# A recurrence with two expert layers on one core: the scans of every second window in another slot, and one PSUM bank emptied in another order

## The chip, the cores and the metric

The kernel runs on one core of a Trainium2 chip. The metric is device time in microseconds (us) of one execution of the program; lower is better. Five engines work side by side, each through its own queue in order: TensorE (PE, its weight loads shown as PEld), VectorE (DVE), ScalarE (ACT), GpSimd (POOL) and SyncE (SP, which here issues the DMA transfers).

## The reference

`r, k, v, w, a, b` have the shape (4, 8, 768, 40): 32 independent (batch, head) pairs, 768 time steps, 40 features. Each pair has a 40x40 state.

```python
for t in range(768):
    y[:, :, t] = einsum('bhd,bhde->bhe', r_t, state)
    Sa = einsum('bhde,bhe->bhd', state, a_t)
    state = state * w_t[:, :, None, :] - outer(Sa, b_t) + outer(v_t, k_t)
x  = y as (3072 tokens, 320)
h  = x @ w_in                                  # 320 -> 1024
s  = h * softmax(h)
x2 = (layer_norm(s) * g_ln) @ w_out            # 1024 -> 320
h2 = x2 @ w_in2                                # 320 -> 2048
out = (max(h2, 0) + alpha * min(h2, 0)) @ w_out2
```

## The kernel before, in words

The 768 steps are cut into 12 windows of 64 steps, and each window into two chunks of 32, so there are 24 chunks. Inside a chunk the recurrence is solved with matrices: the decays are turned into running products by scans along time, keys and values are scaled by them, a strictly triangular 32x32 matrix per pair is formed, its inverse gives the corrections, and the state goes from one chunk to the next.

The program has two phases. **Phase 1** (up to about 743 us of the profiled execution) walks the 24 chunks in 24 *slots*. Slot g computes chunk g (`stage_x`, `stage_u`, `stage_uf`, `stage_st`, `stage_g2`, `stage_s`, `stage_y`, in this order), and beside it the first expert layer of earlier chunks (`mlp_tasks`), the decoding of weights from 64-bit words (`dec`) and the preparation of later windows. **Phase 2** is the second expert layer. The change touches phase 1 alone.

Each four slots form a group; with `W, c4 = divmod(g, 4)` the comments below call c4 = 0 the first slot of a group, c4 = 1 its second, and so on. During group W two windows are prepared, v = 2W+2 and u = 2W+3, which are the four chunks of the next group; for W = 0 to 4 both exist. The preparation of a window has these steps:

- `prep_load` (lines 224 to 230) loads the decays `wt`; `kb_load` (232) loads the keys and b (`kbf`, in two halves); `load_a` (239) clears a part of XS on POOL (line 245) and loads a.
- `check` (250): four ACT passes over the decays that look for values out of range. For windows below 4 it is called from within the scans.
- `prep_scan(w, pe)` (260), once for each half pe: on DVE a clamp (line 279), a small memset, two scans (lines 283 and 287) and a reciprocal between them. They yield the running products H and their inverses F. An odd window makes H first.
- `prep_kb` (304): kbf times F, two DVE products per half (line 309). `prep_a` (312): XS times H, two POOL products per chunk (line 318).
- `gen1(g, half)` (320): 64 PE matmuls per call (line 332) put a chunk's pair products into one PSUM bank, `pg`. After half 1 the bank is emptied in eight pieces of 32x256: four masked products on DVE into XS (line 342), and four negated copies on ACT (line 347), into `lraw` (a part of LMN) or, for chunks 0 to 3, into GR.
- `inverse(W+1)` (350) needs the `lraw` of all four chunks. It begins with a DVE transpose (line 374), goes on as a chain of small DVE products and sums (lines 362, 366, 391), with a part on POOL, and closes with a transpose (395). It is spread over the third and fourth slots of the group. The next group's first slot needs its result in `stage_u` (line 510).
- `trans` (464): PE transposes of kbf, whose copies (472, 473) fill KBS.

The order on PE is the order of the program text. On the other engines the compiler orders the instructions by their place in the text and by what is ready. `fill_tasks` says what goes at which letter within a slot; `slot` calls the letters: a, `pre`, b, `stage_u`, `stage_uf`, c, `stage_st`, `stage_g2` half 0, x, d, `stage_g2` half 1, e, `stage_s`, f, `stage_y`, z. The block `pre` stands right behind `stage_x` and the letter a; its DVE instructions are held behind the last sums of the state (line 550) of the slot before.

Other lines that are spoken of: 550, the DVE sums of the state into VUS, which `stage_s` waits for; 678 (`lnl`), a DVE step between the first expert layer's transposes and its second product (686 to 688, `po`); 691 (`xs`), the ACT copy that empties that product, and 700 (`ptx`), PE transposes of xs, which stand at the head of the next slot's PE queue; 602 and 606, the chunk's output; 714 to 723, decoding of weights (DVE, ACT, DVE, POOL).

Of the kernel before, what the change touches and what calls it, by code (L numbers as in the profile page):

```python
# [12 lines left out]
AF = mybir.ActivationFunctionType  # L13
# [13 lines left out]
NP = 4  # L27
TA, TB = ('0z', '0z', '1a', '1a'), ('2z', '2z', '3a', '3a')
CA, CB = ('3c', '3d'), ('d', 'd')
PA, PB = ('0x','0d','0e','0f'), ('1d','1e','1f','1z')  # L30
RES = 2
LAG, ND4 = 2, 4
PR, SM, TM = (10, 32), 2, 121
DA, KP = (1,), (1,)
PA0, PB0 = ('0x','0d','0e','0f'), ('1d','1e','1f','1z')
TA0 = ('0z', '0z', '1a', '1a')
TAIL = "s2 n0 w2 t0 s1 u0 a0 w3 b0 s1 n1 w4 o0 s1 t1 s1 u1 a1 w5 s1 b1 s1 n2 o1 s1 w6 t2 s1 u2 a2 x w7 s1 b2 s1 n3 o2 s1 t3 s1 u3 b3 s2 o3"
SB, LA, LB, LC, LD, KA, KB = 'd', 'x', 'x', 'c', 'a', 'b', 'b'
DK = (1, 1)
NI = 18  # L40
ZF = (1, 1, 1, 1)
# [7 lines left out]
def tile_kernel(ctx: ExitStack, tc: tile.TileContext, w_fm, a0_fm, a_fm, kb_fm, r_fm, v_fm, v_tm,  # L49
                w1_in, w1_out, g_ln, w2_in, w2_out, alpha, ident_d, mask_d, tri_d, r, k, v, w, a, b, w1_nat, out,  # L50
                manual=True):
    nc = tc.nc
# [59 lines left out]
    GR = ca.tile([128, 32, 48], F32, name="GR")  # L112
# [49 lines left out]
    st = {}  # L162
# [69 lines left out]
    def kb_load(w):  # L232
        kbf = st[w]["kbf"] = b2.tile([104, 16, 2, 2, 32], F32, name="kbf")
        for pe in range(2):
            ss = slice(pe * 8, pe * 8 + 8)
            nc.sync.dma_start(out=kbf[:, ss], in_=kb_fm[w][:, ss])

    def load_a(g):
        w, c = divmod(g, 2)
        x = XS[g % 6]  # L240
        for e, r0 in EO:
            if g < 6:
                nc.sync.dma_start(out=x[0:104, e], in_=a0_fm[g, e])
                continue
            nc.gpsimd.memset(x[64 * e:32 + 96 * e, e], 0.0)
            nc.sync.dma_start(out=x[r0:r0 + 40, e], in_=a_fm[w, c, e])
# [13 lines left out]
    def prep_scan(w, pe):  # L260
        s = st[w]
        wt = s["wt"][pe]
        if w < 4:
            check(w, pe)
        if pe == 0:
            s["F"] = [None, None]
        H3 = s["H"][:, pe * 8:pe * 8 + 8, :]
        Ht = H3.rearrange("p s k -> p (s k)")
        if w < 2:
            wc = m1.tile([104, 521], F32, name="wc", tag=("lnh", "lnl", "Y", "P")[2 * w + pe])  # L270
            Ft = m2.tile([104, 520], F32, name="F", tag="xt")
        else:
            wc = b3.tile([104, 521], F32, name="wc", tag="wf")
            Ft = b3.tile([104, 520], F32, name="F", tag="wf")
        F3 = Ft.rearrange("p (s k) -> p s k", k=65)
        s["F"][pe] = F3
        wv = wt[:, 0:520].rearrange("p (s k) -> p s k", k=65)[:, :, 1:65]
        wz = wc[:, 0:520].rearrange("p (s k) -> p s k", k=65)
        nc.vector.tensor_scalar(out=wz[:, :, 1:65], in0=wv, scalar1=W_MAX, scalar2=W_MIN, op0=ALU.min, op1=ALU.max)
        nc.vector.memset(wc[:, ::65], 0.0)  # L280

        def fwd(d):
            nc.vector.tensor_tensor_scan(out=Ht, data0=wc[:, 0:520], data1=d[:, 0:520], initial=0.0,  # L283
                                         op0=ALU.mult, op1=ALU.add)

        def rev(d):
            nc.vector.tensor_tensor_scan(out=Ft[:, ::-1], data0=wc[:, 520:0:-1], data1=d[:, 520:0:-1],
                                         initial=0.0, op0=ALU.mult, op1=ALU.add)

        if w % 2 == 0:  # L290
            rev(D1)
            nc.vector.reciprocal(out=resets(Dx, 0)[:, :, 0:1], in_=F3[:, :, 0:1])
            fwd(Dx)
            if w:
                if pe == 0:
                    s["rs"] = b1.tile([104, 16], F32, name="rs")
                nc.vector.tensor_tensor(out=s["rs"][:, pe * 8:pe * 8 + 8],
                                        in0=st[w - 1]["H"][:, pe * 8:pe * 8 + 8, 64], in1=F3[:, :, 0], op=ALU.mult)
        else:
            fwd(D1)  # L300
            nc.vector.reciprocal(out=resets(Dx, 1)[:, :, 64:65], in_=H3[:, :, 64:65])
            rev(Dx)

    def prep_kb(w, pe):
        s = st[w]
        for i in range(2):
            o = s["kbf"][:, pe * 8:pe * 8 + 8, :, i, :]
            eng = nc.vector if (i not in KP if w < 2 else DK[w % 2]) else nc.gpsimd
            st["kb1"] = eng.tensor_tensor(out=o, in0=o, in1=s["F"][pe][:, :, 1:65].rearrange("p s (c t) -> p s c t", c=2),  # L309
                              op=ALU.mult)  # L310

    def prep_a(g, *pes):
        w, c = divmod(g, 2)
        x = XS[g % 6]
        for e, r0 in EO:
            o = x[r0:r0 + 40, e, pes[0]:pes[-1] + 1].rearrange("p a s t -> p (a s) t")
            h = st[w]["H"][r0:r0 + 40, pes[0] * 8:pes[-1] * 8 + 8, c * 32:c * 32 + 32]
            (nc.vector if w < 2 and e in DA else nc.gpsimd).tensor_tensor(out=o, in0=o, in1=h, op=ALU.mult)  # L318

    def gen1(g, half):  # L320
        w, c = divmod(g, 2)
        x = XS[g % 6]
        kbf = st[w]["kbf"]
        if half == 0:
            st["pg1"] = ps_at.tile([128, 8, 2, 32], F32, name="pg", tag="at")
        pg = st["pg1"]
        wait(st["slot"], "gen%d%d" % (g % 4, half))
        for p in range(half * 4, half * 4 + 4):
            for pe in range(2):
                for i in range(2):  # L330
                    o = 64 * pe + 32 * i
                    nc.tensor.matmul(pg[o:o + 32, p], lhsT=kbf[:, pe * 8 + p, c, i, :], rhs=x[0:104, :, pe, p, :],
                                     start=True, stop=True)
            pace(0.19, 188)
        if half == 0:
            return
        c4 = g % 4
        for e in range(2):
            q = 64 * e
            for pe in range(2):  # L340
                o = 64 * pe
                nc.vector.tensor_tensor(out=x[q:q + 32, e, pe], in0=pg[o:o + 32, :, e],  # L342
                                        in1=mask[o:o + 32].unsqueeze(1).to_broadcast([32, 8, 32]), op=ALU.mult)
                r = q + 32 * pe
                to = (GR[r:r + 32, c4 * 8:c4 * 8 + 8, 47:15:-1] if g < 4 else
                      st["lraw"][r:r + 32, c4 * 8:c4 * 8 + 8, :])
                nc.scalar.activation(out=to, in_=pg[o + 32:o + 64, :, e], func=AF.Copy, scale=-1.0)  # L347


    def inverse(W):  # L350
# [460 lines left out]
    def fill_tasks(g):  # L811

        W, c4 = divmod(g, 4)
        pre, at = [], {}
        for n, places in ((2 * W + 1, TA if W else TA0), (2 * W + 2, TB)):
            for q, (c, x) in enumerate(places):
                if int(c) == c4 and n < NW:
                    at.setdefault(x, []).append(lambda n=n, q=q: trans(n, q))
        late = []

        def add(q, *fs):
            at.setdefault(q, []).extend(fs)
        w = 2 * W + 4
        if w < NW:
            if c4 == 2:
                add(LA, lambda: prep_load(w), lambda: load_a(2 * w))
            for c, x, pe in ((CA[0][0], CA[0][1], 0), (CA[1][0], CA[1][1], 1)):
                if int(c) == c4 and w > 3:
                    add(x, lambda pe=pe: check(w, pe))
            if c4 == 3:  # L830
                add(LB, lambda: kb_load(w), lambda: load_a(2 * w + 1))
        v = 2 * W + 2
        if c4 == 0 and v < NW:
            pre += [lambda: prep_scan(v, 0), lambda: prep_scan(v, 1)]
            add(KA, lambda: prep_kb(v, 0), lambda: prep_kb(v, 1), lambda: prep_a(2 * v, 0, 1),
                lambda: prep_a(2 * v + 1, 0, 1))
        u = 2 * W + 3
        if u < NW:
            if c4 == 0:
                add(LC, lambda: prep_load(u), lambda: load_a(2 * u))  # L840
                if u > 3:
                    add(CB[0], lambda: check(u, 0))
                    add(CB[1], lambda: check(u, 1))
                add(SB, lambda: prep_scan(u, 0), lambda: prep_scan(u, 1), lambda: prep_a(2 * u, 0, 1))
            if c4 == 1:
                add(LD, lambda: kb_load(u), lambda: load_a(2 * u + 1))
                add(KB, lambda: prep_kb(u, 0), lambda: prep_kb(u, 1), lambda: prep_a(2 * u + 1, 0, 1))
            for n, places in ((2 * W + 2, PA if W else PA0), (2 * W + 3, PB if W else PB0)):
                for f, (c, q) in zip(gen_tasks(n), places):
                    if int(c) == c4:  # L850
                        add(q, f)
        return pre, late, at
# [568 lines left out]
```

## Time and profile before

| | |
|---|---|
| three runs | 1130.83, 1130.81, 1122.72 us |
| median | 1130.81 us |
| the profiled execution | 1134.54 us, of which the span of the trace is 1132.8 us |
| phase 1 | to about 743 us |

A slot is read here from one copy of PX into XP (line 500) to the next; the starts of the 24 copies in the trace are, in us:

| group | first slot | second | third | fourth |
|---|---|---|---|---|
| W = 0 | 44.9 | 99.4 | 136.5 | 163.1 |
| W = 1 | 189.3 | 233.5 | 263.3 | 288.8 |
| W = 2 | 311.2 | 347.4 | 375.9 | 401.6 |
| W = 3 | 427.3 | 463.5 | 496.2 | 519.9 |
| W = 4 | 546.3 | 582.6 | 607.9 | 634.1 |
| W = 5 | 655.7 | 681.2 | 707.0 | 725.6 |

A row of a timeline gives start and duration in us, engine, line, operation, output and inputs, the number of instructions merged, and in brackets how long the engine sat idle before it and what it waited for.

### The profile page before, as it was taken

To read this page: it belongs to the slowest core of one execution; us is meant where nothing else is said; L and a number is where in the kernel's file an instruction comes from. 1 tells how busy PE (TensorE), PEld (TensorE's weight loads), DVE (VectorE), ACT (ScalarE), POOL (GpSimd) and SP (SyncE) were. 2 spreads that over 40 slices of the span, in tenths; PEclk is the share of its full clock that TensorE was granted. 3 is DMA by queue.
4 is the path that set the end of the run, shared out by engine and by line. 5 is a ranking of instruction groups with operands and counts; after the bars stand their busy time and mean duration, and the time that the engine had idled before them with its cause. 6 is when DMAs were issued, how large, how long until landed. Compare 5 with 4: busy or idle time off the path is not lost.

```text
span 1132.8 us, 38016 instructions
## 1 busy us (share of the span) xinstructions
PE 982.7 (87%) x16456; PEld 815.6 (72%) x16456; DVE 740.3 (65%) x1455; ACT 551.9 (49%) x1274; POOL 481.6 (43%) x505
## 2 busy tenths in 40 slices
PE   7777784799878878797878888999999999999997
PEld 3454452677766767576767776888988999999897
DVE  8783899778987788868877955466433333444443
ACT  3446563666757665666476657666212121212121
POOL 6467544453434334443344335245333333333332
PEclk8788787888988888779889989999999999999999
DMA  6443344444334433443334334355102020201000
GB/s 172 105 133 108 102 125 117 98 120 113 85 103 119 113 78 103 111 122 81 100 97 118 110 92 112 111 158 179 36 1 70 1 71 1 70 1 48 1 24 15
DMA packets 104690, 99.74 MB, mean 88 GB/s; under 512 B 38084, under 2 KB 83908, under 8 KB 104516
## 3 DMA queue, kind: packets, MB, share of 16 engines
q1 hardware_dynamic: 104516, 97.24, 31.6%
q8 instruction: 131, 2.15, 0.8%
q14 instruction: 43, 0.35, 0.1%
HBM read 71.78 MB, written 25.43 MB: 86 GB/s over the span
## 4 chain that ended last, share of the span: by engine, by line
PE 50%; DVE 23%; ACT 9%; issue 7%; POOL 5%; DMA 5%; SPq 0%; DVEq 0%; POOLq 0%; ACTq 0%
PE ph L1078 15%; PE acc L1096 5%; PE acc L1097 5%; PE acc L1098 5%; PE h L633 4%; DMA kbf<-in_kb_fm_dram 3%; DVE LMN L366 2%; DVE tmp L362 2%; DVE VUS L550 2%; PE py L598 2%; DVE H L283 2%; PE po L686 2%; PE pf L533 2%; DVE kbf L309 1%; PE po L688 1%
## 5 line engine op out<-in xcount | busy, mean ns | idle before, releaser
L1085 POOL TENSOR_TENSOR gll<-gt,gh 128x512 fp32r<-128x512 f32 (+1 forms) x112 | 128.3, 1146 | 223.7 <-ACT gh L1084 222.6
L653 DVE TENSOR_SCALAR gt<-ph,al 128x512 f32<-128x512 f32 (+1 forms) x112 | 75.5, 674 | 190.1 <-PE ph L1078 189.9
L1084 ACT CAST gh<-gt 128x512 fp32r<-128x512 f32 (+1 forms) x112 | 62.5, 559 | 255.1 <-DVE gt L654 217.0
L633 PE MATMUL h<-w1h,xt 128*128 128x512 f32 x240 | 99.0, 461 | 11.0 <-ACT h L642 11.0
L318 POOL TENSOR_TENSOR XS<-XS,H 40x512 f32<-40x512 f32 (+1 forms) x48 | 66.7, 1395 | 91.5 <-DVE H L283 55.2
L1096 PE MATMUL acc<-w2h,gh 128*128 128x320 f32 x288 | 89.0, 309 | 0.0
L1097 PE MATMUL acc<-w2l,gh 128*128 128x320 f32 x288 | 89.0, 309 | 0.0
L1098 PE MATMUL acc<-w2h,gll 128*128 128x320 f32 x288 | 88.9, 309 | 0.0
L586 POOL TENSOR_TENSOR YS<-YS,mask 64x512 f32<-64x512 f32 x48 | 62.0, 1291 | 55.6 <-ACT YS L585 53.7
L686 PE MATMUL po<-wo1h,lnh 128*128 128x320 f32 x192 | 70.7, 368 | 6.8 <-DVE lnl L678 6.7
L217 PE MATMUL busy<-busy 128*128 128x512 bf16 x231 | 70.2, 458 | 2.2 <-POOL lims L129 1.3
L654 DVE SCALAR_TENSOR_TENSOR gt<-ph,gt 128x512 f32<-128x512 f32 (+1 forms) x112 | 68.8, 615 | 3.7
L688 PE MATMUL po<-wo1h,lnl 128*128 128x320 f32 x192 | 64.6, 336 | 0.2 <-DVE lnl L678 0.2
L562 PE MATMUL pss<-ident,VUS 40*40 40x40 f32 x1472 | 43.8, 217 | 24.1 <-DVE VUS L550 7.7
L633 PE MATMUL h<-w1l,xt 128*128 128x512 f32 x144 | 64.7, 449 | 0.0
L687 PE MATMUL po<-wo1l,lnh 128*128 128x320 f32 x192 | 64.6, 337 | 0.0
L366 DVE TENSOR_TENSOR LMN<-LMN,tmp 128x87 f32<-128x87 f32 (+8 forms) x135 | 60.8, 450 | 2.7
L362 DVE TENSOR_TENSOR tmp<-LMN,LMN 128x87 f32<-128x87 f32 (+8 forms) x135 | 59.9, 443 | 2.7
L562 PEld LDWEIGHTS pss<-ident,VUS 40*40 40x40 f32 x1472 | 37.5, 130 | 33.5 <-issue 14.4
L342 DVE TENSOR_TENSOR XS<-pg,mask 32x256 f32<-32x256 f32 x96 | 40.0, 416 | 32.9 <-ACT LMN L347 23.4
L633 PEld LDWEIGHTS h<-w1h,xt 128*128 128x128 f32 x240 | 47.3, 207 | 18.1 <-ACT h L642 11.1
L1078 PE MATMUL ph<-w1h,w2h 128*128 128x512 f32 x180 | 59.3, 394 | 0.0
(213 smaller groups left out, 2711.6 us busy)
## 6 DMA issues: line engine op xcount, KB each, us to landing
kbf<-in_kb_fm_dram SPq DMA_DIRECT2D x24, 416.0 KB
x2d<-x SPq DMA_DIRECT2D x24, 320.0 KB
xd<-Y SPq DMA_DIRECT2D x24, 256.0 KB
xt<-xd SPq DMA_DIRECT2D x12, 512.0 KB
raw<-in_w_in_dram SPq DMA_DIRECT2D x20, 256.0 KB
wt<-in_w_fm_dram SPq DMA_DIRECT2D x24, 211.7 KB
raw<-in_w_in_dram SPq DMA_DIRECT2D x8, 512.0 KB
raw<-in_w_out_dram SPq DMA_DIRECT2D x16, 256.0 KB
```

What stands on the lines that cost most here:

```text
L362: eng.tensor_tensor(out=tv[:, a - rows[0][0]:b - rows[0][0]], in0=M[:, a:b, s:s + 1].to_broadcast(sh), in1=l.unsqueeze(1).to_broadcast(sh) ...
L366: r = eng.tensor_tensor(out=o, in0=o, in1=tv[:, a - rows[0][0]:b - rows[0][0]], op=ALU.add)
L562: nc.tensor.matmul(p_[o:o + 40, p, :], lhsT=vn[o:o + 40, e, pe * 8 + p, :], rhs=ident[o:o + 40, o:o + 40], start=True, stop=True)
L633: nc.tensor.matmul(st["h"][:, ns], lhsT=l, rhs=r, start=j == 0, stop=j == len(ops) - 1)
L653: nc.vector.tensor_scalar(out=tmp, in0=h, scalar1=0.0, scalar2=al, op0=ALU.min, op1=ALU.mult)
L686: nc.tensor.matmul(po, lhsT=lh[:, k], rhs=wo1h[:, k], start=k == 0, stop=False)
L688: nc.tensor.matmul(po, lhsT=ll[:, k], rhs=wo1h[:, k], start=False, stop=k == K1 - 1)
L1078: nc.tensor.matmul(p, lhsT=l, rhs=r, start=j == 0, stop=j == len(ops) - 1)
L1085: nc.gpsimd.tensor_tensor(out=gll, in0=t, in1=f32(gh), op=ALU.subtract)
L1096: nc.tensor.matmul(acc, lhsT=gh[:, cs], rhs=oh, start=f == 0, stop=False)
L1097: nc.tensor.matmul(acc, lhsT=gh[:, cs], rhs=ol, start=False, stop=False)
L1098: nc.tensor.matmul(acc, lhsT=gll[:, cs], rhs=oh, start=False, stop=f == K2 - 1)
```

## The change

Two edits. The scans of window u (both halves) leave letter d of the group's first slot and stand in `pre` of the second slot. The POOL products of chunk 2u, which stood behind them, go to letter b of the second slot, in front of those of chunk 2u+1. The four `gen1` calls of window u, which stood at d, e, f and z of the second slot, stand at e, f, z and z. The loads and the checks of windows above 3 stay; for window 3 the checks go along with the scans, which call them. In `gen1` the eight pieces of the bank are no longer emptied in turn by DVE and ACT: the four ACT copies come first in the text, then the four DVE products.

```diff
-PA, PB = ('0x','0d','0e','0f'), ('1d','1e','1f','1z')
+PA, PB = ('0x','0d','0e','0f'), ('1e','1f','1z','1z')
...
-PA0, PB0 = ('0x','0d','0e','0f'), ('1d','1e','1f','1z')
+PA0, PB0 = ('0x','0d','0e','0f'), ('1e','1f','1z','1z')
...
         for e in range(2):
             q = 64 * e
             for pe in range(2):
+                o, r = 64 * pe, q + 32 * pe
+                to = (GR[r:r + 32, c4 * 8:c4 * 8 + 8, 47:15:-1] if g < 4 else
+                      st["lraw"][r:r + 32, c4 * 8:c4 * 8 + 8, :])
+                nc.scalar.activation(out=to, in_=pg[o + 32:o + 64, :, e], func=AF.Copy, scale=-1.0)
+        for e in range(2):
+            q = 64 * e
+            for pe in range(2):
                 o = 64 * pe
                 nc.vector.tensor_tensor(out=x[q:q + 32, e, pe], in0=pg[o:o + 32, :, e],
                                         in1=mask[o:o + 32].unsqueeze(1).to_broadcast([32, 8, 32]), op=ALU.mult)
-                r = q + 32 * pe
-                to = (GR[r:r + 32, c4 * 8:c4 * 8 + 8, 47:15:-1] if g < 4 else
-                      st["lraw"][r:r + 32, c4 * 8:c4 * 8 + 8, :])
-                nc.scalar.activation(out=to, in_=pg[o + 32:o + 64, :, e], func=AF.Copy, scale=-1.0)
...
-                add(SB, lambda: prep_scan(u, 0), lambda: prep_scan(u, 1), lambda: prep_a(2 * u, 0, 1))
             if c4 == 1:
+                pre += [lambda: prep_scan(u, 0), lambda: prep_scan(u, 1)]
                 add(LD, lambda: kb_load(u), lambda: load_a(2 * u + 1))
-                add(KB, lambda: prep_kb(u, 0), lambda: prep_kb(u, 1), lambda: prep_a(2 * u + 1, 0, 1))
+                add(KB, lambda: prep_kb(u, 0), lambda: prep_kb(u, 1), lambda: prep_a(2 * u, 0, 1),
+                    lambda: prep_a(2 * u + 1, 0, 1))
```

Here SB was the letter d, LD is a and KB is b.

## Rows read from the trace of the kernel before

**Rows 1.** The page: busy time and share per engine; then the chain's shares by engine

```profile
PE 982.7 (87%) x16456; PEld 815.6 (72%) x16456; DVE 740.3 (65%) x1455; ACT 551.9 (49%) x1274; POOL 481.6 (43%) x505
...
PE 50%; DVE 23%; ACT 9%; issue 7%; POOL 5%; DMA 5%; SPq 0%; DVEq 0%; POOLq 0%; ACTq 0%
```

**Rows 2.** Windows by slot: length; busy PE, PEld, DVE, ACT, POOL; clock; DMA share; GB/s

```profile
44.90:99.40 54.50, 39.95 (x1175) 25.19 (x1173) 45.05 (x81) 27.34 (x61) 30.29 (x20) 0.84 0.36 106
99.40:136.50 37.10, 29.58 (x636) 18.53 (x634) 22.17 (x41) 19.33 (x45) 22.80 (x24) 0.80 0.37 94
...
189.30:233.50 44.20, 28.79 (x654) 23.50 (x655) 35.89 (x74) 26.01 (x59) 22.06 (x22) 0.81 0.38 92
233.50:263.30 29.80, 24.94 (x633) 20.25 (x631) 21.93 (x44) 21.00 (x53) 13.75 (x17) 0.89 0.49 127
...
311.20:347.40 36.20, 26.31 (x643) 22.20 (x642) 30.94 (x58) 21.78 (x56) 17.08 (x18) 0.80 0.35 94
347.40:375.90 28.50, 23.65 (x639) 19.37 (x637) 19.32 (x42) 20.39 (x50) 12.65 (x16) 0.96 0.52 136
...
427.30:463.50 36.20, 26.29 (x643) 22.18 (x642) 30.79 (x57) 21.75 (x55) 17.06 (x18) 0.80 0.35 94
463.50:496.20 32.70, 29.49 (x639) 24.12 (x637) 20.53 (x42) 20.58 (x51) 12.62 (x16) 0.75 0.46 117
...
546.30:582.60 36.30, 26.71 (x645) 21.98 (x644) 30.74 (x58) 21.78 (x56) 17.89 (x18) 0.81 0.35 94
582.60:607.90 25.30, 22.84 (x635) 19.30 (x634) 16.51 (x36) 18.05 (x44) 10.64 (x14) 0.93 0.44 115
```

**Rows 3.** Timeline of DVE, slot 8: start, duration, instruction, idle before and its releaser

```profile
336.44 1.24 DVE L283 TENSOR_TENSOR_SCAN H<-wc,D 104x520 f32<-104x520 f32 x1 [0.27 <-ACT H L257]
...
344.12 2.15 DVE L287 TENSOR_TENSOR_SCAN F<-wc,Dx 104x520 f32<-104x520 f32 x1
```

**Rows 4.** Timeline of ACT in slot 8

```profile
343.10 0.43 ACT L691 COPY xs<-po 128x320 f32<-128x320 f32 x1
```

**Rows 5.** Timeline of PE at the end of slot 8 and into slot 9

```profile
343.58 0.90 PE L700 MATMUL ptx<-ident,xs 128*128 128x128 f32 x3 [6.20 <-ACT xs L691]
344.13 0.78 PE L633 MATMUL h<-w1h,xt 128*128 128x512 f32 x1
...
350.28 0.40 PE L633 MATMUL h<-w1h,xt 128*128 128x512 f32 x1
```

**Rows 6.** Timeline of POOL in slots 8 and 9

```profile
344.00 3.26 POOL L318 TENSOR_TENSOR XS<-XS,H 40x512 f32<-40x512 f32 x2
...
357.74 3.17 POOL L318 TENSOR_TENSOR XS<-XS,H 40x512 f32<-40x512 f32 x2 [7.28 <-DMA XS<-in_a_fm_dram]
```

**Rows 7.** Groups by line, whole kernel (busy, mean ns, idle before)

```profile
L279 DVE TENSOR_SCALAR wc<-wt 104x512 f32<-104x512 f32 x24 | 12.6, 526 | 1.8 <-DMA wt<-in_w_fm_dram 1.8
...
L318 POOL TENSOR_TENSOR XS<-XS,H 40x512 f32<-40x512 f32 (+1 forms) x48 | 66.7, 1395 | 91.5 <-DVE H L283 55.2
```

**Rows 8.** Timeline of DVE in slot 9 and at the start of slot 10

```profile
352.00 0.69 DVE L678 TENSOR_TENSOR lnl<-ptr,lnh 128x512 fp32r<-128x512 f32 x1 [2.41 <-ACT lnh L677]
352.79 1.29 DVE L309 TENSOR_TENSOR kbf<-kbf,F 104x512 f32<-104x512 f32 x2
...
357.55 2.31 DVE L309 TENSOR_TENSOR kbf<-kbf,F 104x512 f32<-104x512 f32 x2 [0.24 <-DMA kbf<-in_kb_fm_dram]
359.89 0.49 DVE L550 TENSOR_TENSOR VUS<-pst,VUS 40x320 f32<-40x320 f32 x1
...
367.00 0.42 DVE L342 TENSOR_TENSOR XS<-pg,mask 32x256 f32<-32x256 f32 x1 [2.19 <-ACT LMN L347]
...
377.80 2.06 DVE L374 STREAM_TRANSPOSE LMN<-LMN 128x1024 f32<-128x1024 f32 x1 [0.69 <-ACT LMN L347]
```

**Rows 9.** Waits, whole kernel (in total, times, longest)

```profile
DVE XS L342 <- ACT LMN L347: 23.4, 22, 2.5
...
ACT GR L347 <- DVE XS L342: 11.0, 9, 3.5
```

More of the change, by code (lines that the diff above doesn't have):

```diff
@@ L34 @@
 DA, KP = (1,), (1,)
-PA0, PB0 = ('0x','0d','0e','0f'), ('1d','1e','1f','1z')
+PA0, PB0 = ('0x','0d','0e','0f'), ('1e','1f','1z','1z')
 TA0 = ('0z', '0z', '1a', '1a')
 TAIL = "s2 n0 w2 t0 s1 u0 a0 w3 b0 s1 n1 w4 o0 s1 t1 s1 u1 a1 w5 s1 b1 s1 n2 o1 s1 w6 t2 s1 u2 a2 x w7 s1 b2 s1 n3 o2 s1 t3 s1 u3 b3 s2 o3"
-SB, LA, LB, LC, LD, KA, KB = 'd', 'x', 'x', 'c', 'a', 'b', 'b'
+LA, LB, LC, LD, KA, KB = 'x', 'x', 'c', 'a', 'b', 'b'
 DK = (1, 1)
```

## The prediction

> **What bounds the kernel now.** I read the page's busy shares first. No engine is full over the whole span: PE is busy 982.7 of 1132.8 us, DVE 740.3 (65%), and the chain that ended last is half PE and a quarter DVE [rows 1]. Such shares mix two phases, so I cut phase 1 into slots with the windows view. There the pattern is plain: the first slots of groups 2, 3 and 4 last 36.2, 36.2 and 36.3 us, the second slots 28.5, 32.7 and 25.3 [rows 2]. In a first slot DVE works 30.9 of 36.2 us and PE 26.3 at a granted clock of 0.80. In a second slot DVE works only 19.3 of 28.5, 20.5 of 32.7, 16.5 of 25.3. So DVE is nearly full in first slots and has 9 to 12 us of slack in second ones.
>
> Then the timelines show what a first slot waits for at its end. In slot 8 the scans of window u run on DVE from 336.44 to 346.27, the last stretched to 2.15 us [rows 3]. ACT takes its queue in order, with pieces that wait for DVE (the decoding, the copies of the bank), so its copy xs starts only at 343.10 [rows 4]. PE sat idle for 6.20 us before the transposes of xs, and comes back at half clock: a matmul of the same form takes 0.78 us at 344.13 and 0.40 at 350.28 [rows 5]. That is the place which the change clears.
>
> **The change part by part.** *The scans leave the first slot.* Per window they are four scans of 1.24 us [rows 3] and two clamps of 0.53 [rows 7]: 4 x 1.24 + 2 x 0.53 = 6.0 us, with the small memsets and reciprocals left out. What this is worth in slot 8 I bound from two sides. By DVE: 30.9 - 6.0 = 24.9 us of work, and with today's idle of 36.2 - 30.9 = 5.3 the slot is 30.2 us, 6.0 shorter. By PE: the 6.20 us of idle goes, and with it the half-clock stretch from 343.6 to the slot's end at 347.4, half of 3.8 = 1.9; together 8.1. I take 7.5, nearer to the PE row because the ending wait is PE's: 3 x 7.5 = 22.5 us for slots 8, 12 and 16, whose windows are alike. Slot 4 lasts 44.2 us with DVE busy 35.9 [rows 2]; it holds other waits too, so I take 5 of a possible 0 to 6. Slot 0 lasts 54.5, DVE 45.1; weight decoding and POOL share its bound, and I take 4 of 0 to 6. Sum: 22.5 + 5 + 4 = 31.5 us gained. What is late next in a first slot is the output of the chunk and its PE products, as in the other slots.
>
> *The scans enter the second slot.* They stand early in the text, ahead of the sums at line 550 and of lnl at 678, and DVE takes its queue in order. In slot 9 the first sum starts at 359.89, 12.5 us after the slot began. Up to there DVE waits 2.41 us before the first lnl and 0.24 for the second half of kbf [rows 8]; that is 2.65 us of cover that the rows name, and both kbf products follow DMAs that do not move. So of 6.0 us some 3.35 stay uncovered. The compiler may start a few scans in idle time at the end of the first slot, where their inputs are ready, and part of what is late there meets slack behind: the slot has 9.2 us of DVE idle in all. Bounds: 0 (all in slack) to 6.0 us per second slot (no cover). I take 2.5 each for slots 5, 9, 13 and 17, and nothing for slot 1, where DVE idles 37.1 - 22.2 = 14.9 us [rows 2]: 10 us lost. Behind a late lnl stand PE's products po and then all of the recurrence's matmuls, which is why I don't take it at 0.
>
> *Two POOL products move along* (1.40 us each [rows 7], 2.8 us per group). In slot 9 POOL idles 7.28 us for a load before its own two [rows 6] and works only 12.65 of 28.5 us [rows 2], so they are hidden behind that load: 0. Without that cover they cost 2.8. No DMA is moved: loads stay at their letters, so SP's queue keeps its order.
>
> *gen1 calls later by one letter.* PE's work is the same. Chunk 2u+1 is made wholly behind `stage_y`; its bank is full at about the same point, since its last half stood at z before. The inverse, which starts when the last ACT copy is done (0.69 us of waiting at 377.80 [rows 8]), should not start later: 0, bounded by +1 per group.
>
> *ACT's four copies first.* Now the eight pieces are taken in turn, each engine waiting for the other: DVE waits 23.4 us in 22 places for ACT's copies, and ACT waits 11.0 us in nine places for DVE in the first four banks alone [rows 9]. In slot 9 one such wait is 2.19 us [rows 8]. With copies first there is one handover instead of seven. Most of it is off the path, because DVE and ACT have slack there. On the path are the first four banks (the opening inverse waits for them) and the start of each inverse. Bounds: 10 us gained to 4 lost (DVE's four masks stand together behind all copies, and could hold up a chunk). I take 2 gained.
>
> Sum: -31.5 + 10 + 0 + 0 - 2 = -23.5 us, made against the profiled execution's 1134.5 (1132.8 of span and 1.7 around it): 1111.0. The median of the runs stands 3.7 us below that execution; the same saving from 1130.8 gives 1107.3, and I forecast **1107**.
>
> **The rivals.** *The second slot takes it all back.* If nothing covers the scans, each of five second slots grows by 6.0 us, 30 in all, against 31.5 + 2 gained: 1127. For it: the scans stand ahead of everything in the slot. Against it: 7.9 us or more of DVE idle in each second slot [rows 2].
>
> *Slower: PE stalls in the second slot and the inverse starts late.* PE's order is fixed; if the kbf and XS products end after PE has reached letter e, it stops at gen1, with `stage_s` and `stage_y` behind it, and its clock falls as at 344.13 [rows 5]. Price per group: 6.0 for the scans, 2.8 for two more POOL products in front of gen1, 2 for half clock, 10.8 in all, 54 over five groups, against 33.5 gained: 1151. It decides from the point where XS of chunk 2u is ready later than the last sum at line 550. Against it: XS products would end about 6 us after kbf's second half, which is near that point but still ahead of the later letter.
>
> *POOL and DVE get in each other's way.* The last scan of slot 8 took 2.15 us, not 1.24, as POOL's products ran from 344.00; the kbf pair at 357.55 took 2.31, not 1.29, beside POOL's at 357.74 [rows 3, 6, 8]. With four POOL products in a row in the second slot, 2.8 us more of them lie beside DVE's work, and 0.9 us of stretching leaves the first slot: 1.9 per group, 9.5 in all: 1117. [...]
>
> *The change does not do what it says.* The compiler could place the scans in the first slot's end all the same, as their inputs are ready there: then only gen1's order counts, and the time is about 1129. Against it: in the text they now stand behind that slot's whole chain.
>
> **How the numbers follow.** Chances: the forecast 0.60, POOL against DVE 0.14, taken back 0.11, late inverse 0.09, not moved 0.06. About 1% (11 us) is what a measurement can tell here, as the three runs lie 8 us apart; faster by more means below 1119.5. That holds for nearly all of the forecast (0.58) and most of the POOL case (0.10): 0.68; same 0.23, which is the rest of these two, the case of all taken back and that of nothing moved; slower by over 1% is the late inverse: 0.09. The forecast's own range is 1092 to 1120. The low end of the range is the best of each bound: 3 x 8.1 + 6 + 6 in first slots and 8 of gen1's 10 give 44 us, 1087; the high end takes in the case of all taken back: 1130.
>
> **What would show it.** Right: the windows of slots 8, 12 and 16 near 28 to 30 us with a granted clock above 0.85; no wait of PE for xs near 6 us; scans on DVE between the second slot's start and its kbf products; second slots 1 to 4 us longer; few waits between lines 342 and 347. Wrong: second slots over 34 us, PE waiting in front of line 332 or for lnl by more than 4 us, the transpose at line 374 later after its slot's start, or scans that still lie at the end of first slots.

## Result and the profile after: slower by 1.2%

The changed kernel takes 1141.78 us in the median of four runs (1140.55 to 1143.68), the kernel before 1129.80 in four beside it. The ratio is 1.0121, interval 1.0076 to 1.0166. The forecast was 1107 with a range up to 1130: wrong in sign. The profiled execution took 1140.73 us, 1138.9 of it span.

The page of the changed kernel: busy time per engine, and the chain's shares by engine.

```profile
PE 980.4 (86%) x16435; PEld 817.0 (72%) x16459; DVE 741.3 (65%) x1455; ACT 552.1 (48%) x1274; POOL 474.6 (42%) x505
...
PE 47%; DVE 25%; ACT 9%; issue 7%; POOL 5%; DMA 4%; SPq 0%; POOLq 0%; DVEq 0%; ACTq 0%
```

Against [rows 1] nothing stands out: the same work, placed otherwise. So I cut phase 1 by slots: first and second slots of groups 1 to 4, columns as in [rows 2].

```profile
189.60:231.10 41.50, 27.04 (x643) 21.47 (x644) 33.04 (x68) 26.00 (x59) 18.68 (x21) 0.79 0.40 97
231.10:266.00 34.90, 30.07 (x644) 24.52 (x644) 18.40 (x37) 19.75 (x49) 13.35 (x16) 0.75 0.37 94
315.40:350.80 35.40, 26.17 (x645) 21.41 (x645) 30.56 (x59) 21.77 (x55) 15.31 (x17) 0.86 0.38 99
350.80:381.70 30.90, 24.92 (x637) 20.33 (x636) 19.07 (x38) 19.95 (x50) 12.54 (x17) 0.89 0.43 119
429.00:464.50 35.50, 25.49 (x651) 20.95 (x650) 30.59 (x59) 21.72 (x56) 15.38 (x17) 0.90 0.40 100
464.50:498.80 34.30, 26.10 (x632) 21.41 (x630) 19.03 (x38) 19.82 (x50) 12.58 (x17) 0.75 0.39 105
545.70:582.40 36.70, 26.79 (x649) 22.32 (x648) 30.58 (x60) 21.71 (x55) 15.35 (x17) 0.87 0.36 97
582.40:613.70 31.30, 25.11 (x634) 20.60 (x632) 18.70 (x38) 19.94 (x50) 11.87 (x15) 0.83 0.41 111
```

The four first slots sum to 149.1 us against 152.9 in [rows 2]; the forecast wanted 27.5 off. The four second slots sum to 131.4 against 116.3: 15.1 us lost, of which 9.8 is more idle time of PE and 5.3 more busy time (PE's busy column sums to 106.2 against 100.9), at a lower granted clock in three of the four (0.75, 0.89 and 0.83 in slots 5, 9 and 17 against 0.89, 0.96 and 0.93). The third and fourth slots of these groups gave back 7.1 us (190.2 against 197.3), and the profiled execution of the kernel before is 4.7 us above its median; so the two profiles lie only 6.2 us apart, and the windows tell where the time moves better than how much. And DVE's work in first slots is unchanged, 30.56 us in slot 8 against 30.94. The scans did not leave. DVE's timeline at the end of slot 8:

```profile
340.27 1.24 DVE L283 TENSOR_TENSOR_SCAN H<-wc,D 104x520 f32<-104x520 f32 x1 [1.18 <-ACT H L257]
...
348.03 2.15 DVE L287 TENSOR_TENSOR_SCAN F<-wc,Dx 104x520 f32<-104x520 f32 x1
350.20 0.42 DVE L708 TENSOR_TENSOR x<-ptx,x 128x256 fp32r<-128x256 f32 x1
```

The first scan starts 24.9 us into its slot, before 25.2 [rows 3]. Moving them in the text held them only behind sums that are done by then; their inputs are ready, and the built program has them at the end of the first slot all the same. The end of the slot, on ACT and then on PE:

```profile
343.25 0.51 ACT L720 ACTIVATE em<-em,ebias 128x256 int32<-128x256 int32 x1 [0.69 <-DVE em L718]
...
345.80 0.42 ACT L695 COPY xs<-po 128x320 f32<-128x320 f32 x1
...
350.66 0.26 ACT L709 CAST x<-ptx 64x128 fp32r<-64x128 f32 x1 [1.70 <-DVE x L708]
350.82 0.42 ACT L504 COPY XP<-px 128x320 f32<-128x320 f32 x1
```

```profile
346.28 0.90 PE L704 MATMUL ptx<-ident,xs 128*128 128x128 f32 x3 [5.94 <-ACT xs L695]
```

PE's wait for xs is 5.94 us, as long as the 6.20 of [rows 5]. From 337.91 to xs ACT waits only those 0.69 us: it is working its queue off: checks of the decays (line 257), weight decoding (em), the chunk's output (Y), copies into KBS. One part did what it says: the handovers between the two emptying lines.

```profile
DVE XS L349 <- ACT LMN L344: 9.9, 7, 2.9
```

With 3.3 us more in one wait for GR, 13.2 us in eight waits against 25.7 in 24 (the 23.4 in 22 of [rows 9], and 2.3 in two for GR); and ACT's waits for the masks are gone. Now slot 9, where time was lost: SP, DVE, PE.

```profile
354.36 0.80 SPq L236 DMA_DIRECT2D kbf<-in_kb_fm_dram  x2
```

```profile
358.72 1.29 DVE L309 TENSOR_TENSOR kbf<-kbf,F 104x512 f32<-104x512 f32 x2 [2.75 <-DMA kbf<-in_kb_fm_dram]
...
364.53 0.99 DVE L554 TENSOR_TENSOR VUS<-pst,VUS 40x320 f32<-40x320 f32 x2
365.44 1.21 DVE L644 SCALAR_TENSOR_TENSOR P<-h,P 128x1024 f32<-128x1024 f32 x1
...
368.49 0.99 DVE L554 TENSOR_TENSOR VUS<-pst,VUS 40x320 f32<-40x320 f32 x2
```

```profile
365.67 0.81 PE L566 MATMUL pss<-ident,VUS 40*40 40x40 f32 x32 [0.92 <-DVE VUS L554]
369.63 0.76 PE L566 MATMUL pss<-ident,VUS 40*40 40x40 f32 x16 [3.16 <-DVE sm L649]
...
371.28 0.47 PE L690 MATMUL po<-wo1h,lnh 128*128 128x320 f32 x1
371.55 0.47 PE L691 MATMUL po<-wo1l,lnh 128*128 128x320 f32 x1
```

The kbf products begin 7.9 us into the slot, 5.4 before [rows 8]; they end at 12.1 us, 12.5 before, but the reduce of the activation (line 642, 1.21 us), which stood between the two pairs of products before, now stands behind them, ahead of the sums. The last of the four sums ends 18.7 us into the slot, 16.6 before. The two pairs of sums stand 4 us apart with the P product and weight decode between, and PE stands 3.16 us in the middle of pss, the transposes of the new state (the row names sm, DVE's small step right behind the last sum). The matmuls behind that wait start 0.27 us apart, about half as fast as the po matmuls from 360.32 to 361.34, 0.15 us apart. In slots 5, 9, 13 and 17 together the idle time ahead of pss matmuls is 16.3 us; before it was 1.8. From here "pss wait" means this sum of the bracketed waits in PE's timeline.

### The profile page after: what moved, and what is told of

Same layout as the page of the kernel before. It is cut to its first block, busy times and chain, and to the rows that moved or that the text cites. A ratio compares the mean times of both kernels' runs of the same rounds, so it can differ in the third digit from the quotient of the medians.

```text
span 1138.9 us, 38018 instructions
## 1 busy us (share of the span) xinstructions
PE 980.4 (86%) x16435; PEld 817.0 (72%) x16459; DVE 741.3 (65%) x1455; ACT 552.1 (48%) x1274; POOL 474.6 (42%) x505
## 3 DMA queue, kind: packets, MB, share of 16 engines
q8 instruction: 131, 2.15, 0.8%
## 4 chain that ended last, share of the span: by engine, by line
PE 47%; DVE 25%; ACT 9%; issue 7%; POOL 5%; DMA 4%; SPq 0%; POOLq 0%; DVEq 0%; ACTq 0%
PE ph L1083 15%; PE acc L1101 5%; PE acc L1102 5%; PE acc L1103 5%; PE h L637 3%; DVE LMN L370 3%; DVE VUS L554 3%; DVE tmp L366 3%; DMA kbf<-in_kb_fm_dram 2%; PE py L602 2%; PE po L690 2%; PE po L692 1%; DVE H L283 1%; PE pss L566 1%; PE po L691 1%
## 5 line engine op out<-in xcount | busy, mean ns | idle before, releaser
L657 DVE TENSOR_SCALAR gt<-ph,al 128x512 f32<-128x512 f32 (+1 forms) x112 | 75.5, 674 | 190.4 <-PE ph L1083 190.2
L637 PE MATMUL h<-w1h,xt 128*128 128x512 f32 x240 | 101.6, 472 | 9.3 <-ACT h L646 9.3
L318 POOL TENSOR_TENSOR XS<-XS,H 40x512 f32<-40x512 f32 (+1 forms) x48 | 63.7, 1331 | 92.2 <-DVE H L283 58.6
L590 POOL TENSOR_TENSOR YS<-YS,mask 64x512 f32<-64x512 f32 x48 | 65.5, 1365 | 69.7 <-ACT YS L589 67.7
L566 PE MATMUL pss<-ident,VUS 40*40 40x40 f32 x1472 | 48.3, 224 | 34.0 <-DVE VUS L554 15.6
L566 PEld LDWEIGHTS pss<-ident,VUS 40*40 40x40 f32 x1472 | 40.9, 136 | 44.5 <-issue 23.0
L217 PE MATMUL busy<-busy 128*128 128x512 bf16 x206 | 61.5, 450 | 6.3 <-issue 4.4
L370 DVE TENSOR_TENSOR LMN<-LMN,tmp 128x87 f32<-128x87 f32 (+8 forms) x135 | 63.4, 470 | 3.0
L366 DVE TENSOR_TENSOR tmp<-LMN,LMN 128x87 f32<-128x87 f32 (+8 forms) x135 | 57.6, 427 | 2.6
L727 POOL TENSOR_TENSOR dec<-em 128x256 f32<-128x256 f32 x36 | 27.2, 755 | 69.9 <-DVE em L724 42.4
```

The lines of the kernel that those rows point to most:

```text
L366: eng.tensor_tensor(out=tv[:, a - rows[0][0]:b - rows[0][0]], in0=M[:, a:b, s:s + 1].to_broadcast(sh), in1=l.unsqueeze(1).to_broadcast(sh) ...
L370: r = eng.tensor_tensor(out=o, in0=o, in1=tv[:, a - rows[0][0]:b - rows[0][0]], op=ALU.add)
L566: nc.tensor.matmul(p_[o:o + 40, p, :], lhsT=vn[o:o + 40, e, pe * 8 + p, :], rhs=ident[o:o + 40, o:o + 40], start=True, stop=True)
L637: nc.tensor.matmul(st["h"][:, ns], lhsT=l, rhs=r, start=j == 0, stop=j == len(ops) - 1)
```

## The experiments

The ratio given for each run is against the kernel before on the same chip, with its interval. The first four runs are to decide between three theories. A: the scans stayed where they were, and the changed order in gen1 (its letters and the emptying of its bank) is what costs time. B: the new place of the scans and of the POOL products in the text reorders the kbf loads and products. C: the letters of the gen1 calls alone carry the loss.

### Which part of the change costs the time

**Order of emptying alone**, the kernel before with the four ACT copies in a loop ahead of the four masks:

```diff
+ for e, pe: nc.scalar.activation(out=to, in_=pg[o + 32:o + 64, :, e], ...)
  for e, pe:
      nc.vector.tensor_tensor(out=x[q:q + 32, e, pe], ...)
-     nc.scalar.activation(out=to, in_=pg[o + 32:o + 64, :, e], ...)
```

> Only the order in which gen1's bank is emptied, four copies of ACT first; scans and letters as before. Theory A (the scans did not really move; the loss is in the second slots, from the changed gen1): slower than before by 3 to 8 us, second slots 2 to 5 us longer, the second pair of the state's sums 1 to 2 us later. Rival B (the loss comes from the scans' and POOL products' new place in the text, which reorders the loads of kbf): faster by 2 to 5 us, as the forecast's term for this edit had it. Rival C (the letters of gen1 cost it): within 2 us of before.

1127.62 us, 1.0004 (0.9981 to 1.0027); pss wait 1.6. This part costs and gives nothing.

**All but the order**: the change with the old emptying in turn.

> The scans, the POOL products and gen1's letters as in the change; the bank emptied in turn, as before. Theory A: about as before, 1126 to 1134. Rival B: slower by 8 to 14 us, all of the loss. Rival C: slower by 8 to 12 us too; the next run tells it from B.

1134.04 us, 1.0036 (0.9994 to 1.0078). Most of the loss is gone although the letters are the new ones. That speaks against B, and against C as it stands: new letters do not always cost 8 to 12 us. In three of its four second slots VectorE's sums are not parted two and two by the P product, as they are in the changed kernel, and in slot 9 the last of them ends 14.8 us into the slot; pss wait 3.3.

**Letters alone**, the kernel before with one edit:

```diff
- PB = PB0 = ('1d','1e','1f','1z')
+ PB = PB0 = ('1e','1f','1z','1z')
```

> Before, with gen1's four calls for window u at e, f, z and z of the second slot in place of d, e, f and z; nothing else. Theory A and rival B: within 3 us of before. Rival C: slower by 8 to 12 us, with the second slots 2 to 5 us longer.

1143.93 us, 1.0148 (1.0101 to 1.0194), pss wait 12.7. The letters alone cost as much as the whole change, as C had it. Not all of it lies in the second slots: against the profile before, slots 5, 9, 13 and 17 are 4.2 us longer together and slots 4, 8, 12 and 16 10.8, while the fourth slots are shorter by 5.4. The same from the other side:

**The change with the old letters.**

> The change with its four letters of the second group's gen1 calls set back to d, e, f, z; scans' text place and the order of emptying stay changed. Theory T1 (the letters take one of two gen1 halves away from in front of the state transposes, pss, and TensorE then stands about 3 us there in slots 5, 9, 13, 17): back to 1124-1132, no wait over 1 us within pss in slot 9. Rival T4 (the loss needs the scans' new place too, and stays without the letters): 1136-1142.

1128.69 us, 1.0003 (0.996 to 1.0046), pss wait 3.7. Taking the letters out takes the loss out.

### By what the letters cost it

PE's timeline of slot 9 shows the difference: before, both gen1 halves of the first chunk (64 matmuls) stand between pst (the products that VectorE's sums take up) and pss; with the new letters one does (32; in the trace one gen1 call is 32 matmuls, and 64 are a chunk's two calls), and PE arrives at pss earlier than VectorE's sums. Before, then the changed kernel:

```profile
360.04 0.71 PE L332 MATMUL pg<-XS,kbf 104*32 104x64 f32 x30
...
362.67 0.66 PE L332 MATMUL pg<-XS,kbf 104*32 104x64 f32 x30
363.26 0.65 PE L562 MATMUL pss<-ident,VUS 40*40 40x40 f32 x24
```

```profile
364.22 0.53 PE L332 MATMUL pg<-XS,kbf 104*32 104x64 f32 x20 [0.89 <-issue]
```

Two of the runs above show what the half in front is worth. With the order of emptying alone VectorE's sums in slot 9 are as late as in the changed kernel (the last ends 19.1 us into the slot, against 18.7) and parted two and two, and kbf goes out as late (3.5 us into the slot in both). But both halves stand in front of pss, and PE hardly waits:

```profile
360.33 0.99 DVE L554 TENSOR_TENSOR VUS<-pst,VUS 40x320 f32<-40x320 f32 x2
...
364.32 0.99 DVE L554 TENSOR_TENSOR VUS<-pst,VUS 40x320 f32<-40x320 f32 x2
```

```profile
365.46 0.81 PE L566 MATMUL pss<-ident,VUS 40*40 40x40 f32 x32 [0.44 <-DVE sm L649]
```

That run is at 1.0004, and the change with the old letters, with the last sum of slot 9 at 18.6 us, at 1.0003. So in these two late sums cost nothing with both halves in front, and one half in front cost little where the sums were early (all but the order, 1.0036). The loss of over 1% came where the two met: in the change and with the letters alone. Three other sets of letters in the changed kernel:

```diff
- ('1e','1f','1z','1z')
+ ('1e','1e','1f','1z')   first run
+ ('1d','1e','1z','1z')   second run
+ ('1d','1f','1z','1z')   third run
```

> The change with letters e, e, f, z: both halves of the first chunk behind the second g2 half, but both still in front of pss. T1 (only the count of gen1 halves in front of pss matters): 1124-1133, slots 9, 13, 17 at 28 to 32, 29 to 33, 25 to 28. Rival T3 (what matters is that a half lies between the two g2 halves, where it covers the wait for the kbf products): 1137-1143 as with the changed letters. Rival T2 (the late end of the second group costs it): as T1 here, since f and z are the old places.

1134.38 us, 1.0075 (1.0041 to 1.0109), pss wait 4.7: between T1 and T3. With both halves ahead of pss PE waits little there, though VectorE still parts the sums two and two in three of the four slots; yet half of the loss stays, and no run explains it.

> The change with letters d, e, z, z: both halves of the first chunk back in front of pss, both of the second chunk at the slot's end, as in the change. T1: 1124-1133. Rival T2 (the second chunk's late halves, with their masks and copies running into the next slot, are the cost): 1136-1143, with slots 6, 10, 14, 18 or the second slots' ends longer. T3: as T1.

1124.67 us, 0.9953 (0.9916 to 0.9989), pss wait 5.0. The late second chunk is cleared.

> The change with letters d, f, z, z: the first half back between the g2 halves, the second one behind pss as in the change. T1 (one half only in front of pss): the loss stays, 1136-1143, with a wait of 2 to 3 us within pss in slot 9. T3 (a half between the g2 halves is what matters): 1124-1133. T2 (late second chunk): 1136-1143, but without the wait within pss.

1126.72 us, 0.9971 (0.9934 to 1.0008), although only one half stands ahead of pss, and PE does wait there (10.6 us in all, 1.44 of it once in slot 9). By time T1 falls here: the count of halves is not enough, and neither is the pss wait a measure of the loss. What else differs is VectorE's order, in three of the four slots three sums and one instead of two and two; in slot 9 the last sum ends 16.0 us into the slot:

```profile
365.06 1.52 DVE L554 TENSOR_TENSOR VUS<-pst,VUS 40x320 f32<-40x320 f32 x3
366.61 1.23 DVE L644 SCALAR_TENSOR_TENSOR P<-h,P 128x1024 f32<-128x1024 f32 x1
367.82 0.47 DVE L554 TENSOR_TENSOR VUS<-pst,VUS 40x320 f32<-40x320 f32 x1
```

So two edits aim at the sums. **kbf's load placed a slot earlier in the text**, in the changed kernel:

```diff
- add(LD, lambda: kb_load(u), lambda: load_a(2 * u + 1))
+ add(LD, lambda: load_a(2 * u + 1))
- add(LC, lambda: prep_load(u), lambda: load_a(2 * u))
+ add(LC, lambda: prep_load(u), lambda: load_a(2 * u), lambda: kb_load(u))
```

> The change with one edit: the load of the second group's kbf is issued in the first slot instead of at the start of the second. Theory V1 (in the changed kernel VectorE stands 2.75 us at kbf for its DMA in slot 9, and all that is queued behind, the sums too, is late): no wait for the kbf DMA, the four second slots' waits of TensorE within pss fall from 16 us together to under 8, 1128-1136. Rival V2 (VectorE's own order, with the reduce, the P product and the weight decode between the pairs of sums, keeps the sums late): waits within pss stay at 11 us or more, 1137-1143.

1124.04 us, 0.9961 (0.9926 to 0.9997); pss wait 9.8: 0.6 and 1.2 us in slots 5 and 13 (26.2 and 25.8 us long), still 4 us each in slots 9 and 17. Neither theory named this. The load did not come into the first slot: on SP's queue it goes out 0.7 us into slot 9, 2.9 us earlier than in the change, and VectorE still waits 2.15 us for it. An earlier load takes the loss away here; as the run with the order of emptying alone loads as late as the change and loses nothing, a late load alone is not the loss.

**Sums first**: in second slots the activation chain (reduce, Exp, P product) is issued behind all four sums.

```diff
  stage_st(g, 0); stage_st(g, 1)
+ st["sums"] = g
+ if "rest" in st:
+     with tc.issue_after(st["fence"].ins): st.pop("rest")()
...
- solu_norm(st["h"], P, st["sm", t])
+ if st.get("sums") == st["slot"] or st["slot"] % 4 != 1: solu_norm(h, P, m)
+ else: st["rest"] = lambda: solu_norm(h, P, m)
```

First in the changed kernel:

> The change with one edit: in the second slot of each four the activation chain (reduce, P product) is issued behind all four sums, so that VectorE's order is kbf products, four sums, then reduce and P product. V2: waits within pss in slots 5, 9, 13, 17 fall from 16 us together to under 6, slots 9 and 17 to 27 to 29, and 1126-1135. V1 (kbf's DMA is what is late): pss waits stay over 9, 1135-1142.

1127.76 us, 1.0045 (1.0011 to 1.0079), pss wait 2.8. Then, as a control, in the kernel before:

> Control: the kernel before with the activation chain issued behind all four sums in the second slots, gen1's letters as they were. If late sums are what the letters cost (V2), there is little to win here, since TensorE waits only 1.8 us in all within pss in slots 5, 9, 13 and 17 of the kernel before: 1122-1132. If putting the sums first is worth time in itself (rival V3), it wins as much here as in the changed kernel: 1112-1118.

1134.47 us, 1.0052 (1.0027 to 1.0077). And in the kernel before with the new letters alone:

> The kernel before with the changed letters alone (which took 1143.9) and the activation chain issued behind all four sums. V2: the waits within pss in the four second slots fall from 12.7 us to under 6, and the time to 1126-1134. Rival (the letters cost it by something else, such as gen1 work that ends later): 1138-1146.

1130.58 us, 1.0046 (1.0016 to 1.0076), pss wait 2.3. Its slot 9, DVE and then PE:

```profile
355.37 0.49 DVE L550 TENSOR_TENSOR VUS<-pst,VUS 40x320 f32<-40x320 f32 x1
356.78 0.48 DVE L550 TENSOR_TENSOR VUS<-pst,VUS 40x320 f32<-40x320 f32 x1
357.97 0.99 DVE L550 TENSOR_TENSOR VUS<-pst,VUS 40x320 f32<-40x320 f32 x2
358.88 1.21 DVE L638 TENSOR_REDUCE sm<-h 128x1 f32<-128x1024 f32 x1
```

```profile
358.98 1.11 PE L562 MATMUL pss<-ident,VUS 40*40 40x40 f32 x48
...
361.54 0.50 PE L562 MATMUL pss<-ident,VUS 40*40 40x40 f32 x16
```

With the sums first, the new letters cost nothing (1.0046 against 1.0052 with the old); without, they cost 1.5%. The edit is no gain in itself: it costs the kernel before half a per cent. Against the letters alone it takes, in the profiles, 10.2 us out of the four second slots and 3.9 out of the first ones. With the runs that have late sums and both halves in front, this shows that the letters lose their time where the sums are late. It does not show that the wait at pss is the whole of the price: with 10.6 and 9.8 us of it two runs lost nothing (0.9971 and 0.9961).

### What ends the first slots

**Scans really held in the second slot**, in the changed kernel:

```diff
- with tc.issue_after(st["fence"].ins):
+ with tc.issue_after((st.get("held", st["fence"]) if g % 4 == 1 else st["fence"]).ins):
      for f in pre: f()
...
+ st["held"] = nc.vector.tensor_tensor(out=x2[64:128, 4], ...)   in tr2
```

> The change, and in addition DVE's scans of window u in the second slot are held behind the slot's first DVE work (the second half of x2), so that they cannot run in the first slot. In the change's own trace they still run there from 340.3 to 350.2 us in slot 8. If the forecast's sum was right and only the premise failed (the scans never moved): first slots 8, 12 and 16 of 28 to 30 us in place of 35.5, second slots 2 to 5 us longer than the change's, the whole 1112 to 1128. If the second slot has no room for them: first slots shorter all the same, second slots 7 us longer, the whole 1138 to 1146. If the first slot's length is not due to the scans: first slots stay at 34 to 36, the whole 1150 or more.

1141.08 us, 1.0137 (1.0078 to 1.0196), pss wait 18.8. Here the scans stand behind x, and DVE's work in slot 8 falls to 23.14 us; yet slots 8, 12 and 16 last 34.8, 35.5 and 34.4, as if their length were not due to the scans. Then **xs of first slots copied by VectorE**, in the kernel before:

```diff
- nc.scalar.copy(out=xs, in_=po)
+ if st["slot"] % 4 == 0: nc.vector.tensor_copy(out=xs, in_=po)
+ else: nc.scalar.copy(out=xs, in_=po)
```

> The kernel before with one edit: in the first slot of each four the copy xs is made by VectorE, not ScalarE. Theory U1 (two chains of nearly the same length end the first slot: ScalarE's full queue up to xs, and VectorE's scans up to x, on which the last x copy and XP wait): TensorE's wait for xs in slot 8 falls from 6.2 to under 3 us, but XP still comes late behind x, so slots 8, 12, 16 stay at 34 to 38 us and the time at 1122-1134. Rival U2 (ScalarE's queue alone sets the end): slots 8, 12, 16 fall to 29 to 32 and the time to 1108-1118.

1130.72 us, 1.0035 (1.0001 to 1.0068); slots 8, 12, 16 at 34.0, 36.3, 35.2. **Scans held, old letters, xs on ScalarE:**

> The change with the scans held in the second slot and the old letters, xs left on ScalarE: of the two chains that end the first slots only VectorE's scans are taken away. U1 (either chain alone holds the slot): slots 8, 12, 16 stay at 33.5 to 36 us with a wait of 5 us for xs, and the time is 1124-1136. Rival (the gain of the version with both edits comes from the held scans alone): slots 8, 12, 16 at 32 to 33 and 1116-1122.

1123.69 us, 0.9975 (0.9944 to 1.0007); slots 35.0, 35.6, 35.0. PE waits for xs as long as ever, with no scan ahead of it:

```profile
335.54 0.90 PE L704 MATMUL ptx<-ident,xs 128*128 128x128 f32 x3 [6.12 <-ACT xs L695]
```

**Both: scans held and xs on VectorE, old letters.**

> The change with the scans really held in the second slot, its gen1 letters set back to d, e, f, z, and xs in the first slots copied by VectorE: both chains taken away at once. U1: slots 8, 12, 16 fall to 28 to 32; the second slots, which now carry 6 us of scans ahead of their sums, take back 2 to 4 us each; 1115-1128. U2 (ScalarE's queue alone): the same first slots, so e9 tells U1 from U2. Rival U3 (the first slot is bound by the sum of VectorE's and TensorE's work, not by a chain): first slots stay at 33 or more, 1128-1140.

1119.26 us, 0.9931 (0.9898 to 0.9964): faster than both kernels. Its slots 8, 12 and 16, by windows, and ACT at the end of slot 8:

```profile
306.60:340.00 33.40, 25.41 (x652) 20.99 (x651) 23.09 (x48) 20.93 (x53) 13.51 (x17) 0.95 0.34 93
420.90:453.00 32.10, 25.66 (x652) 20.87 (x651) 23.04 (x48) 20.90 (x53) 13.50 (x17) 0.95 0.36 96
533.90:566.00 32.10, 25.58 (x651) 20.72 (x650) 23.27 (x49) 20.89 (x53) 13.51 (x17) 0.94 0.37 96
```

```profile
333.19 0.71 ACT L257 ACTIVATE H<-wt,lims 104x512 f32<-104x512 f32 x1
...
337.35 0.28 ACT L476 COPY KBS<-pt 64x160 f32<-64x160 f32 x1
...
339.76 0.37 ACT L710 CAST x<-ptx 128x256 fp32r<-128x256 f32 x1
340.03 0.43 ACT L504 COPY XP<-px 128x320 f32<-128x320 f32 x1
```

Over slots 8, 12 and 16 either edit alone takes 3 us (108.6 to 105.5 and 105.7), both together 10.9 (97.6). Only the last is clear: in the kernels here with neither edit this sum lies anywhere from 106.1 to 117.7 us, and in the four with both at 96.4 to 98.6. The run with xs alone keeps the old emptying and the old place of the POOL products, so it differs from the one with both in these too. That is U1 in its numbers, but not in its whole mechanism. In the run with xs alone on VectorE, XP did not wait for x:

```profile
343.59 0.43 ACT L500 COPY XP<-px 128x320 f32<-128x320 f32 x1
```

```profile
345.19 0.42 DVE L707 TENSOR_TENSOR x<-ptx,x 128x256 fp32r<-128x256 f32 x1
```

XP stood at the end of ScalarE's queue, where four checks take 2.9 us and eight KBS copies 2.3. In the version with both edits ACT's rows show no wait from 323.2 to 340.0. So I read the end of a first slot as ScalarE's in-order queue; that is argued from the rows, as the only run that takes work out of that queue alone, the one with xs, gained 3 us. The scans add only the waits of that queue for VectorE (2.4 us in slot 8 of the changed kernel: 0.69 and 1.70). The changed kernel's trace shows queues kept in order: on ScalarE XP follows at 350.82 right behind the cast that waited 1.70 us, though PE had turned from px to other work by 348.76; VectorE stood idle for 2.75 us up to the kbf products at 358.72, and lnl, whose lnh ScalarE had done at 357.88, came behind them at 359.93.

### Going on from the faster version

Three runs started from the one at 1119.26: kbf loaded early; that and the sums first; the letters d, e, z, z.

> The version with scans held in the second slot, xs of the first slots on VectorE and old letters (1119.3), with the second group's kbf loaded in the first slot. In that version TensorE waits 2 to 3 us a second slot at gen1 for the kbf products and the loads; if the load is the late one, 1112-1118; if VectorE's place for the products behind the held scans is, no change, 1117-1123.

1121.19 us, 0.9931 (0.9901 to 0.9960): no change.

> As the run before it, with the activation chain issued behind the four sums too. Little wait is left within pss in that version (0.9 us in four slots), so V2 expects no more than 1 to 3 us below the run before it; V3 (sums first wins in itself) expects 8 to 12 below.

1119.31 us, 0.9922 (0.9897 to 0.9946): no more than V2 allowed.

> The version with held scans and xs on VectorE (1119.3), with the letters d, e, z, z that were the best of the four sets tried in the change (1124.7 against 1128.7 with the old ones). If that difference carries over, 1113-1118; if it belonged to the order in which the other kernel was laid out, 1117-1123.

1126.02 us, 0.9988 (0.9953 to 1.0022): by its median worse than the old letters here, with intervals that just overlap. The set that was the fastest in the change is not so here; I take it that a set of letters has no value of its own, but is good or bad with the order that VectorE comes out with.

## Why the prediction was wrong

**What bounds the kernel now.** The rows were right, the reading was not. "ACT takes its queue in order, with pieces that wait for DVE" made VectorE the culprit for the late xs. Over the same stretch ScalarE was working: its waits are some 2 us, and with the scans gone the 6 us wait for xs stayed (6.12).

**The scans leave the first slot: -31.5.** They did not leave: the last rival, given 0.06, is what happened. Its argument against ("behind that slot's whole chain") failed, since text order binds only through what the fence and the inputs hold. But the term was wrong also where the scans do leave. The 7.5 us a slot lay between two bounds, 6.0 from VectorE's work with today's idle kept, and 8.1 from PE's wait for xs, which was to go with the scans. That wait stayed at 6.12 us. In the run with scans held and the old letters slots 8, 12 and 16 fell by 1.1, 0.5 and 1.2 us; with xs moved too, by 2.7, 4.1 and 4.1.

**The scans enter the second slot: +10.** Where they truly entered, with the old letters, slots 5, 9, 13 and 17 sum to 115.3 us against 116.3, and with xs moved too to 119.2: from nothing to 0.7 us a slot, near the lower bound and not the 2.5 taken.

**gen1 later by one letter: 0, at most +1 per group.** This is the step that turned the sign. It asked for the bank and the inverse, and not what the matmuls had covered while they stood in front of pss. Letters alone cost 1.5%, some 17 us, over three times the bound, and taking them out of the change takes its loss out (1.0003). The slower rival came near in kind (PE stalls in the second slot at a lower clock) but put the stall in front of gen1 for lack of kbf products; it was in pss for lack of sums (with the letters alone, slot 9 has both: 2.4 us in front of gen1's matmuls and 3.8 in pss).

**"No DMA is moved".** In the text, yes. On SP's queue kbf was issued at 354.36, behind x2d and od, 3.5 us into the slot with both halves; before, the first half went out 1.2 us into it. The first pair of kbf products and the sums moved with it. In the run with the order of emptying alone the same late load costs nothing, so this premise was false but did not by itself set the sign.

**ACT's four copies first: -2.** The handovers fell as forecast and the time did not: 1.0004. Yet in the change it has a part: with the old emptying the sums come earlier and the ratio is 1.0036. Two POOL products, and POOL against VectorE, were not tried by themselves; the stretched scan (2.15 us) is still there.

The forecast's rival at 1129 was right on the scans and missed the time by 13 us; with the old letters in place the change comes back to the kernel before (1.0003), so the miss is the letters, together with the late sums. Two of the forecast's own signs of being wrong came: scans at the end of first slots, and second slots over 34 us (34.9 and 34.3).

What remains open: how the 1.2% divides between the late kbf load and VectorE's order between the sums, as either edit alone brings the time back; why the letters alone lengthen first slots; why the letters e, e, f, z keep half of the loss with both halves in front of pss; and moving the four checks out of first slots was not tried. Sets of letters that differ in one place moved the time by 0.5 to 0.6% in either direction, with intervals that overlap (0.9953 against 1.0003 in the change, 0.9988 against 0.9931 in the version with both edits), so differences of half a per cent between these kernels are not explained one by one.

## What to carry to other kernels

Before moving work that looks free on its own engine, ask which wait of the next in-order consumer it had been covering: here 32 matmuls in front of a step were, by the runs with late sums and both halves in front, the cover for another engine's sums. When one engine waits for another, look whether the other is waiting or working; only waits go away by removing work elsewhere. And a move in the program's text is no move until the order of the built program shows it; hold it with a dependency, or count it as not made.

## What was not expected of the hardware

PE's granted clock fell after quite short stops, here of 1.12 and 1.28 us. In the kernel with the letters alone, PE's timeline in slot 9, from gen1's matmuls on:

```profile
358.21 0.30 PE L332 MATMUL pg<-XS,kbf 104*32 104x64 f32 x2 [1.12 <-DVE kbf L309]
359.80 1.06 PE L332 MATMUL pg<-XS,kbf 104*32 104x64 f32 x26 [1.28 <-DVE kbf L309]
362.45 1.29 PE L562 MATMUL pss<-ident,VUS 40*40 40x40 f32 x32 [1.59 <-DVE VUS L550]
365.92 1.17 PE L562 MATMUL pss<-ident,VUS 40*40 40x40 f32 x16 [2.18 <-DVE VUS L550]
...
367.72 0.47 PE L688 MATMUL po<-wo1h,lnl 128*128 128x320 f32 x1
367.99 0.47 PE L686 MATMUL po<-wo1h,lnh 128*128 128x320 f32 x1
```

The granted clock there is 1.00 from 352.0 to 359.7 and 0.50 from 359.9 to 370.0; over the slot, 347.2 to 377.2, its mean is 0.83. So it fell before the waits at pss, at the end of the second of two waits for the kbf products, 1.12 and 1.28 us, with two matmuls between them. The po matmuls start 0.27 us apart, while those ahead of gen1 start 0.145 apart. For nine matmuls that is 9 x 0.125 = 1.1 us on top of the 3.8 us of waiting at pss. In the changed kernel's slot 9 it fell later, inside the wait of 3.16 us: 1.00 from 351.0 to 367.8, 0.50 from 368.1 to 374.6.
